# A decoder step of two layers with a KV cache: another root for the layer norms, a closing norm in one pass, and another order and form of the weight loads

## The chip, the cores and the metric

The kernel runs on one core of a Trainium2 chip. Times are device microseconds (us) of one launch, from the start of the program to its end. The core has five engines with queues of their own: PE (TensorE, matrix products), DVE (VectorE), ACT (ScalarE), POOL (GpSimd) and SP (SyncE, which here only issues DMAs). They meet through semaphores. All DMAs of the core share 16 DMA engines.

## What is computed

There are 8 sequences (batches) with one new token each, a model width of 512, 32 query heads of 128 on 8 key/value heads, and caches of 8192 positions in bfloat16. An attention block and a dense block are applied twice, with the same weights and the same caches:

```
def attention(x):                       # x: [8, 1, 512]
    q = x @ wq                          # wq: [512, 4096]
    scores = q . k_cache * 128 ** -0.5  # k_cache: [8, 8, 8192, 128]
    o = softmax(scores) . v_cache       # v_cache: [8, 8, 8192, 128]
    return o @ wo                       # wo: [4096, 512]

def dense(x):
    return silu(x @ w1) @ w2            # w1: [512, 1792], w2: [1792, 512]

layernorm(x) = (x - mean(x)) / sqrt(var(x) + 1e-5)

for layer in (0, 1):
    x = x + attention(layernorm(x))
    x = x + dense(layernorm(x))
```

The caches hold 268 MB. What the second layer reads again must be loaded again, unless it was kept on the chip.

## The kernel before

**Tasks and positions.** The work is cut into 128 tasks, one for each layer, batch and key/value head. A task has 8 positions of 1024 cache rows; position p belongs to task p // 8. K and V come in granules of 512 KB (two positions each). At each position PE transposes a part of K with an identity matrix (`emit_t`, L527; DVE or ACT copies the result back, L535 and L533), multiplies queries with K (`emit_s`, L566), and, 12 positions later, weights with V (`emit_pv`, L632). The softmax of a task lies between: a maximum on DVE (L577), an all-reduce over the partitions on POOL (L581), the exponential on ACT (L591), another all-reduce (L599), a transposition on PE (L607).

**The arena.** Cache granules live in an arena of 28 slots. The 20 granules of K of a batch that belong to heads 3 to 7 (the "kept" ones) have homes in slots 8 to 27: they stay, transposed, from layer 0 to layer 1 of a batch, whose tasks for these heads follow each other closely. So the order of tasks is 3 heads and 5 kept heads of batch 0, three heads of the next batches, the 5 kept heads of batch 0 in layer 1, and so on.

**The planner.** `plan_loads` puts all cache loads into a heap ordered by need, the position that first wants the data. It takes the loads out one by one and gives each a slot. The key for choosing prefers a slot that comes free at least 10 us (in the planner's own clock) ahead of the need, then the least waste, then the slot that comes free last. A load of several granules that finds no such slot is split. Each load gets `after`, the position at which its slots are free (-2: from the start). A slot with a home may be lent out only if the home's next load comes 10 us or more after the lent slot is free.

**The queue.** SP issues the loads strictly in the planner's order. After the commands of position p, `issue_until(p)` issues the loads at the head of the queue whose `after` is at most p; the first one that is not yet due holds up all behind it. At the start (L502 to L506) come the four granules of task 0, then `wq`, then what `after` = -2 allows at the head of the queue (two granules), then `wo`, `w1` and `w2` in one go. The input x is the first DMA of SP's queue (L464).

**Layer norm.** `normed` (L692) is used twice, at the opening (with wq) and at the closing (with w1). It sums x over the partitions (`total`, L674 on DVE and L676 on POOL), subtracts the mean (L680), starts the product with the weights on PE (L728), and meanwhile computes the sum of the squares of the centred x, again with an all-reduce. `inverse_root` (L652) then gets the inverse root on DVE: a guess by integer arithmetic (3 instructions) and three Newton steps (9 instructions). `scaled` (L710) multiplies the product by it.

**Chains.** For each batch, when its last head of layer 0 is done, `chain_of` (L817) takes that one batch from attention to the queries of layer 1: `wo`, residual, norm, `w1`, Silu by exponential and reciprocal, `w2`, residual, norm, `wq`. It is a list of steps, of which one or two are emitted at each position, beside the attention of other batches. The norms' stages (`ln_stages`, L684) lie beside pieces of the products: `ask` for the first heads is cut into as many pieces as the norm has stages. Before the first chain, from position 24, `column_sums` (L807) multiplies wq and w1 by ones.

**Closing.** `closing` (L765) handles the last dense block for all batches: residual (L759), rows by PE (L771), `normed` with w1, each product repeated four times over, six filler matmuls (`keep_busy(AFTER)`, L547), scaling (L710), Silu on ACT (L784), w2 on PE (L771), a copy (L788) and four DMAs (L966). A small Silu ahead of it (L778) makes ACT load the table for it.

Of the kernel before, what the change touches and what calls it, by code (L numbers as in the profile page):

```python
# [6 lines left out]
HQ = 32  # L7
DH = 128
SM_SCALE = DH ** -0.5
LN_EPS = 1e-5  # L10
RSQRT_SEED = float(0x5F3759DF)
NEWTON = 3

GRP = 8
GPT = 8
# [18 lines left out]
W1PARTS = 7  # L34
W2PARTS = 4
QSOON = 3
ASKS = (2, 5)
SUMS = 24
NTP = 3
NSCP = 2  # L40
NQB = 2
NST = 2
# [3 lines left out]
PVN = (12, 16)  # L46
CW = 32
AGAIN = 4
BEFORE, AFTER = 4, 6
ACT_EVAC = (0, 4, 6)  # L50

BF16 = mybir.dt.bfloat16
FP32 = mybir.dt.float32
INT32 = mybir.dt.int32
ACT = mybir.ActivationFunctionType
ALU = mybir.AluOpType
AX = mybir.AxisListType
# [140 lines left out]
def plan_loads(tasks, kept, nslot, ngran):  # L198
# [9 lines left out]
    heap = []  # L208
# [17 lines left out]
    for i, (layer, b, g) in enumerate(tasks):  # L226
# [11 lines left out]
        for ks in split(list(range(ngran)), wide):  # L238
            push("V", i, tuple(ks))

    def lead(need, after):
        return clock[max(0, need)] - clock[after] if after >= 0 else FAR

# [2 lines left out]
    loads = []  # L246
    while heap:
        d = heapq.heappop(heap)[-1]
        n = len(d.ks)
        if d.home is not None:  # L250
            for m in range(n):
                reserved[d.home + m].pop(0)
        else:
            best = None
            for slot in range(nslot - n + 1):
                held = free[slot:slot + n]
                if any(r and lead(r[0], f) < AHEAD for r, f in zip(reserved[slot:slot + n], d.free)):
# [35 lines left out]
def _build(ctx, nc, A_x, A_k_cache, A_v_cache, A_wq, A_wo, B_w1, B_w2, out):  # L293
# [67 lines left out]
    Xr = P  # L361
# [2 lines left out]
    Pf = P[:, :].bitcast(FP32)  # L364
    halves = (1 + FT + 1) // 2
    assert NST == 2 and 2 * KT <= FT <= HQ
    small = sb([128, 4 * B + 4 * REP * NST + USED + 2 * FT + 2 * HQ + NST + 1 + halves], FP32, "small")
    taken = [0]

    def cut(n):  # L370
        taken[0] += n
        return small[:, taken[0] - n:taken[0]]

    yr, tr, s1, s1a = [cut(B) for _ in range(4)]
# [85 lines left out]
    with nc.Block() as block:  # L460

        @block.sync
        def _(sync_eng):
            dma(sp, Xr[0:B, :], x_in, wsem["x"], writes=["P"])  # L464

            op(pool, lambda: pool.memset(ident[:, :], 1.0), writes=["ident"])
            op(
# [4 lines left out]
                ),  # L472
                reads=["ident"], writes=["ident"],
            )
            for n in range(NQB):
                op(pool, lambda n=n: pool.memset(QB[n], 0.0), writes=[f"QB{n}"])
            op(dve, lambda: dve.memset(one, 1.0), writes=["one"])
# [8 lines left out]
               reads=["hm"], writes=["far"])  # L486

            queue = list(loads)

            def issue_until(pos):  # L490
                while queue and queue[0].after <= pos:
                    issue(queue.pop(0))
# [4 lines left out]
            def load_rest():  # L497
                dma(sp, wo_sb[:, :, :], A_wo.rearrange("(h p) d -> p h d", p=128), wsem["wo"], writes=["wo"])
                dma(sp, w1_sb[:, :, :], B_w1.rearrange("(kt p) f -> p kt f", p=128), wsem["w1"], writes=["w1"])
                dma(sp, w2_sb[:, :, :], B_w2.rearrange("(ft p) d -> p ft d", p=128), wsem["w2"], writes=["w2"])  # L500
# [141 lines left out]
            def emit_norm(ti):  # L642
# [4 lines left out]
                else:  # L647
                    dst, rd = QA[:, b * HQ + g * REP:b * HQ + (g + 1) * REP], f"QA{b}"
                op(dve, lambda: dve.tensor_tensor(dst, OTp[ob][:, 0:REP * width_of(ti):width_of(ti)], rcp[st], ALU.mult),
                   reads=[f"OT{ob}", f"rcp{st}"], writes=[rd])  # L650

            def inverse_root(n):  # L652
                v, y, t = s1a[:, 0:n], yr[:, 0:n], tr[:, 0:n]
                vi, yi = v.bitcast(INT32), y.bitcast(INT32)

                def guess():
                    op(dve, lambda: dve.tensor_scalar(v, v, 1.0 / D, LN_EPS, op0=ALU.mult, op1=ALU.add),
                       reads=["s1a"], writes=["s1a"])
                    op(dve, lambda: dve.tensor_scalar(yi, vi, 1, None, op0=ALU.logical_shift_right),
                       reads=["s1a"], writes=["yr"])  # L660
                    op(dve, lambda: dve.tensor_scalar(yi, yi, -1.0, RSQRT_SEED, op0=ALU.mult, op1=ALU.add),
                       reads=["yr"], writes=["yr"])

                def newton():
                    op(dve, lambda: dve.tensor_tensor(t, y, y, ALU.mult), reads=["yr"], writes=["tr"])
                    op(dve, lambda: dve.scalar_tensor_tensor(t, t, -0.5, v, op0=ALU.mult, op1=ALU.mult),
                       reads=["tr", "s1a"], writes=["tr"])
                    op(dve, lambda: dve.scalar_tensor_tensor(y, t, 1.5, y, op0=ALU.add, op1=ALU.mult),
                       reads=["tr", "yr"], writes=["yr"])

                return [guess] + [newton] * NEWTON

            def total(xv, rx, n):
                op(dve, lambda: dve.tensor_reduce(s1[:, 0:n], xv.rearrange("p k b -> p b k"), AX.X, ALU.add),  # L674
# [17 lines left out]

                return [lambda: total(xv, rx, 1), second] + inverse_root(1)

            def normed(xv, rx, w_sb, rw, outs, again=1):

                total(xv, rx, B)
                center(xbB, ["PT", "xb"], xv, rx, B)
                for f in project(w_sb, rw, outs, KT, lambda k: xbB[:, k, :], "xb", B, again=again):
                    f()  # L700
                if again > 1:
                    keep_busy(AFTER)
# [12 lines left out]
            def project(w_sb, rw, outs, kparts, rhs_of, r_rhs, n, parts=1, again=1):  # L715

                steps = []
                w = CW if n == 1 else n * again

                def moved(k):  # L720
                    if n == 1:
                        return rhs_of(k).to_broadcast([128, w])
                    return rhs_of(k).unsqueeze(1).to_broadcast([128, again, n]) if again > 1 else rhs_of(k)

                for i, o in enumerate(outs):
                    for k in range(kparts):
                        steps.append(
                            lambda i=i, o=o, k=k: pe.matmul(  # L728
                                MISC[:, i * n:i * n + w] if again == 1 else
                                MISC[:, i * w:(i + 1) * w].rearrange("p (r b) -> p r b", b=n),  # L730
                                w_sb[:, k, o * 128:(o + 1) * 128], moved(k),
                                start=(k == 0), stop=(k == kparts - 1),
                            )
                        )
# [30 lines left out]
            def closing(x0, x1, r0, r1):  # L765
# [3 lines left out]
                def quads(lhs_of, rhs_of, parts, first, last):  # L769
# [14 lines left out]
                op(act, lambda: act.activation(hsB, hB, ACT.Silu), reads=["P"], writes=["hsB"])  # L784
# [32 lines left out]
            def chain_of(b):  # L817
# [179 lines left out]
```

## Time and profile before

| what | value |
|---|---|
| median of 3 runs | 1169.84 us (1167.94 to 1170.11) |
| the profiled execution: time, and its span | 1167.9 us, 1166.2 us |
| busy: PE, weight loads, DVE, ACT, POOL | 965.2, 753.7, 597.4, 382.7, 117.7 us |
| read from HBM | 465.05 MB, 399 GB/s over the span |
| granted PE clock, mean | 0.969 |
| cache loads: V of 512 KB, V of 1 MB, K of 512 KB, K of 1 MB, K of 2 MB | 284, 114, 192, 32, 24 |
| K and V copies out of transposition: DVE, ACT | 690 ns x 440, 1011 ns x 264 |

How to read it: busy time is a share of the span for each engine, and several engines work at once, so the shares don't add up to the time. The page has the span in 40 slices with the share of busy time as a digit from 0 to 9, and for the DMA engines the rate. The chain of work that ended last is followed back from the last instruction, at each step to what released it. In a timeline each line has a start, a duration, the engine, the line of the kernel, the operation, what it writes and reads, the number of instructions, and in brackets the idle time ahead of it with what ended it; "issue" there means that the profile shows nothing that the engine waited for. Times in a timeline count from the start of the span.

### The profile page before, as it was taken

Reading aid. Unit: us, or ns where it says so; the run is one execution under the profiler, and the core shown is the slowest. Engines: PE = TensorE matmul, PEld = TensorE weight load, DVE = VectorE, ACT = ScalarE, POOL = GpSimd, SP = SyncE. Lnnn points to the kernel's source line nnn. Section 1 sums busy time; section 2 is a strip of 40 time slices with the busy share of each in tenths; the row PEclk is TensorE's granted clock in tenths of the full one; section 3 lists DMA queues with packets and bytes.
Section 4 is the critical chain, followed back from the end, with each engine's and each line's share of the span. In section 5 each row is a group of like instructions: output and inputs, shape, how many; then the busy total and the mean of one; then the engine's idle time right before and its main releaser. Section 6 shows DMA issues by size and latency. Waiting matters only on the chain.

```text
span 1166.2 us, 44949 instructions
## 1 busy us (share of the span) xinstructions
PE 965.2 (83%) x19898; PEld 753.7 (65%) x19898; DVE 597.4 (51%) x1932; ACT 382.7 (33%) x660; POOL 117.7 (10%) x300
## 2 busy tenths in 40 slices
PE   4478888798879887888878988989889888888786
PEld 3367666576657675667656766767667665767564
DVE  2235654455535563556545654556445553556444
ACT  1133331343223431443223431343233422443232
POOL 0000111000110111001110111001100011001110
PEclk8799999999998999999999999899989999999999
DMA  9999999999999999999999999999999999999995
GB/s 346 393 417 378 385 407 412 420 413 402 410 422 405 404 398 417 421 407 399 407 423 411 389 406 422 420 404 396 414 422 412 396 409 420 420 382 406 412 411 214
DMA packets 100274, 467.98 MB, mean 401 GB/s; under 512 B 10472, under 2 KB 16368, under 8 KB 77808
## 3 DMA queue, kind: packets, MB, share of 16 engines
q1 hardware_dynamic: 100048, 465.10, 99.2%
q8 instruction: 157, 2.57, 0.9%
q14 instruction: 37, 0.30, 0.1%
q10 hardware_dynamic: 32, 0.00, 0.0%
HBM read 465.05 MB, written 0.01 MB: 399 GB/s over the span
## 4 chain that ended last, share of the span: by engine, by line
DMA 55%; PE 32%; DVE 5%; issue 4%; ACT 2%; SPq 1%; POOL 1%; POOLq 0%; ACTq 0%; DVEq 0%
DMA arena<-in_A_v_cache_dram 28%; DMA arena<-in_A_k_cache_dram 26%; PE TPp L527 12%; PE OTp L632 9%; PE SCp L566 6%; PE MISC L728 3%; ACT P L591 2%; PE TPp L607 2%; DVE small L577 2%; PE MISC L747 1%; DVE arena L535 1%; SPq L432 1%; POOL small L581 1%; DVE PT L611 0%; DVE small L579 0%
## 5 line engine op out<-in xcount | busy, mean ns | idle before, releaser
L527 PE MATMUL TPp<-ident,arena 128*128 128x128 bf16 x5632 | 444.9, 223 | 86.4 <-DMA arena<-in_A_k_cache_dram 80.7
L535 DVE COPY arena<-TPp 128x1024 bf16<-128x1024 bf16 x440 | 303.6, 690 | 311.9 <-PE TPp L527 309.7
L527 PEld LDWEIGHTS TPp<-ident,arena 128*128 128x128 bf16 x5632 | 330.8, 99 | 152.5 <-DMA arena<-in_A_k_cache_dram 99.1
L533 ACT COPY arena<-TPp 128x1024 bf16<-128x1024 bf16 x264 | 266.9, 1011 | 313.3 <-PE TPp L527 313.2
L632 PE MATMUL OTp<-PT,arena 128*128 128x64 bf16 (+1 forms) x8192 | 319.5, 191 | 56.9 <-DMA arena<-in_A_v_cache_dram 29.9
L632 PEld LDWEIGHTS OTp<-PT,arena 128*128 128x128 bf16 x8192 | 275.2, 98 | 96.6 <-issue 52.8
L566 PE MATMUL SCp<-arena,QB 128*32 128x512 bf16 x2048 | 208.6, 398 | 11.7 <-DVE arena L535 5.8
L591 ACT ACTIVATE P<-SCp,small 128x512 bf16<-128x512 f32 x128 | 87.9, 687 | 383.7 <-DVE small L587 218.5
L581 POOL PARTITION_ALL_REDUCE small<-small x128 | 47.5, 371 | 718.9 <-DVE small L579 691.6
L577 DVE TENSOR_REDUCE small<-SCp 128x1 f32<-128x512 f32 x128 | 87.5, 684 | 40.6 <-PE SCp L566 39.7
L566 PEld LDWEIGHTS SCp<-arena,QB 128*32 128x32 bf16 x2048 | 54.3, 93 | 59.6 <-DVE arena L535 9.6
L599 POOL PARTITION_ALL_REDUCE small<-small x128 | 55.8, 436 | 235.3 <-DVE small L597 235.3
L611 DVE COPY PT<-TPp 128x256 bf16<-128x256 bf16 x128 | 37.3, 292 | 81.4 <-PE TPp L607 81.4
L607 PE MATMUL TPp<-ident,P 128*128 128x128 bf16 x512 | 51.3, 223 | 24.4 <-ACT P L591 24.3
L607 PEld LDWEIGHTS TPp<-ident,P 128*128 128x128 bf16 x512 | 29.2, 98 | 57.3 <-ACT P L591 44.9
L597 DVE TENSOR_SCALAR small<-small 128x4 f32<-128x4 f32 x128 | 29.1, 228 | 31.4 <-ACT P L591 30.3
L728 PE MATMUL MISC<-XT,wq 128*128 128x32 bf16 x1024 | 39.9, 177 | 1.4 <-issue 1.3
L728 PEld LDWEIGHTS MISC<-XT,wq 128*128 128x128 bf16 x1024 | 32.2, 96 | 9.0 <-issue 9.0
L747 PE MATMUL MISC<-at,wo 128*128 128x32 bf16 x1024 | 35.8, 176 | 0.9 <-issue 0.9
L747 PEld LDWEIGHTS MISC<-at,wo 128*128 128x128 bf16 x1024 | 31.5, 96 | 4.8 <-issue 4.8
L579 DVE SCALAR_TENSOR_TENSOR small<-small 128x4 f32<-128x4 f32 x128 | 28.5, 223 | 4.5
L585 DVE SCALAR_TENSOR_TENSOR small<-small 128x4 f32<-128x4 f32 x128 | 19.9, 156 | 20.4 <-POOL small L581 20.4
(69 smaller groups left out, 321.1 us busy)
## 6 DMA issues: line engine op xcount, KB each, us to landing
arena<-in_A_v_cache_dram SPq DMA_DIRECT2D x284, 512.0 KB, 8.2
arena<-in_A_v_cache_dram SPq DMA_DIRECT2D x114, 1024.0 KB, 11.5
arena<-in_A_k_cache_dram SPq DMA_DIRECT2D x192, 512.0 KB, 8.2
arena<-in_A_k_cache_dram SPq DMA_DIRECT2D x24, 2048.0 KB, 14.0
arena<-in_A_k_cache_dram SPq DMA_DIRECT2D x32, 1024.0 KB, 12.8
wq<-in_A_wq_dram SPq DMA_DIRECT2D x1, 4096.0 KB, 16.9
wo<-in_A_wo_dram SPq DMA_DIRECT2D x1, 4096.0 KB, 30.4
w<-in_B_w_dram SPq DMA_DIRECT2D x2, 1792.0 KB, 25.2
```

The lines of the kernel that those rows point to most:

```text
L527: lambda c=c: pe.transpose(tpv[:, c, :], chunk(slot, h * GRP + c), ident[:, :])
L533: op(act, lambda: act.copy(dst, TPp[tb][:, :]), reads=[f"TP{tb}"], writes=[r_half(slot, h)])
L535: op(dve, lambda: dve.tensor_copy(dst, TPp[tb][:, :]), reads=[f"TP{tb}"], writes=[r_half(slot, h)])
L566: lambda c=c: pe.matmul(SCp[bank][c * QUAD:(c + 1) * QUAD, :], QB[qn][:, NGRAN - 1 - k:NGRAN - 1 - k + QUAD], ARENA[:, slot * SLOT + c * K ...
L577: op(dve, lambda: dve.tensor_reduce(rowmax, SCp[bank][:, :], AX.X, ALU.max), reads=[f"SC{bank}"], writes=["rowmax"])
L581: op(pool, lambda: pool.partition_all_reduce(tops, top, 128, bass.bass_isa.ReduceOp.max), reads=["top"], writes=["tops"])
L591: op(act, lambda: act.activation(P[:, :], SCp[bank][:, :], ACT.Exp, bias=shift, scale=SM_SCALE, accum_out=rs[st]), reads=[f"SC{bank}", "sh ...
L599: op(pool, lambda: pool.partition_all_reduce(ssa[st], ssm[st], 128, bass.bass_isa.ReduceOp.add), reads=[f"ssm{st}"], writes=[f"ssa{st}"])
L607: lambda c=c: pe.transpose(tpv[:, c, :], P[:, c * 128:(c + 1) * 128], ident[:, :])
L632: lambda c=c, cc=cc: pe.matmul(otp, chunk(slot, h * GRP + c), pv[:, cc % CPB, cc // CPB % NQ, k, :].unsqueeze(2).to_broadcast([128, REP, w ...
L728: lambda i=i, o=o, k=k: pe.matmul(MISC[:, i * n:i * n + w] if again == 1 else MISC[:, i * w:(i + 1) * w].rearrange("p (r b) -> p r b", b=n ...
L747: lambda o=o, h=h: pe.matmul(MISC[:, o * w:(o + 1) * w], wo_sb[:, h, o * 128:(o + 1) * 128], rhs_of(h).to_broadcast([128, w]) if n == 1 el ...
```

## The change

- Every inverse root becomes exp(-0.5 ln(v)) on ACT, behind one DVE instruction that forms the variance. ACT loads, at the start, a table that holds both Ln and Exp. The chains' norms have four stages for six; the pieces of `ask` stay six.
- The closing's norm is done in one pass: ACT squares x, DVE sums x and the squares, and one all-reduce on POOL takes both sums. POOL then forms the offset and the centred x itself, two operations of kinds that it does not have elsewhere. Three DVE instructions form the variance. Two filler matmuls come ahead of w1's product, five behind it. The last Silu becomes Exp on ACT and three operations on DVE.
- w2 is loaded with two of its rows side by side in a partition (packets of 2 KB for 1 KB). To match, w1's columns are read with a step of two.
- wo, w1 and w2 go into the planner's heap at positions 16, 30 and 48 instead of into the queue at the start. The loads of the first three tasks take the slot that is free earliest; as `after` is the first part of this key, their loads of V are always split into single granules.
- x is loaded by ACT's queue.

```diff
+WEIGHTS = (("wo", 16), ("w1", 30), ("w2", 48))
-BEFORE, AFTER = 4, 6
+BEFORE, BETWEEN, AFTER = 4, 2, 5
...
+    for kind, need in WEIGHTS:
+        heapq.heappush(heap, (need, kind, 0, (), Load(kind, 0, 0, 0, (), need, [], None)))
...
+        if n == 0:
+            d.after = -2
+            loads.append(d)
+            continue
...
+                elif d.task < OPENING:
+                    key = (after, waste, 0, slot)
...
-            dma(sp, Xr[0:B, :], x_in, wsem["x"], writes=["P"])
+            dma(act, Xr[0:B, :], x_in, wsem["x"], writes=["P"])
...
+            act.add_instruction(mybir.InstLoadActFuncSet(
+                name=nc.get_next_instruction_name(), act_func_set_id=LN_EXP, ins=[], outs=[]))
...
+                        if d.kind == "w2":
+                            dst = dst[:, :, :].rearrange("p (a c) d -> p a (c d)", c=FC)
+                            src = src.rearrange("(a p c) d -> p a (c d)", p=128, c=FC)
...
-            load_rest()
...
+            def root(n):
+                op(act, lambda: act.activation(tr[:, 0:n], s1a[:, 0:n], ACT.Ln), reads=["s1a"], writes=["tr"])
+                op(act, lambda: act.activation(yr[:, 0:n], tr[:, 0:n], ACT.Exp, scale=-0.5), reads=["tr"], writes=["yr"])
...
-                return [guess] + [newton] * NEWTON
+                return [shifted, lambda: root(n)]
...
+                def columns(k, o):
+                    if rw == "w1":
+                        lo = o // FC * FC * 128 + o % FC
+                        return w_sb[:, k, lo:lo + FC * 127 + 1:FC]
+                    return w_sb[:, k, o * 128:(o + 1) * 128]
...
-                op(act, lambda: act.activation(raw[:, 0:1], raw[:, 0:1], ACT.Silu), reads=["raw"], writes=["raw"])
...
-                normed(x1, r1, w1_sb, "w1", range(FT), AGAIN)
+                op(act, lambda: act.activation(sqB, x1, ACT.Square), reads=[r1], writes=["PT", "sqB"])
+                op(dve, lambda: dve.tensor_reduce(s1, x1.rearrange("p k b -> p b k"), AX.X, ALU.add),
+                   reads=[r1], writes=["two"])
+                op(dve, lambda: dve.tensor_reduce(two[:, B:2 * B], sqB.rearrange("p k b -> p b k"), AX.X, ALU.add),
+                   reads=["sqB"], writes=["two"])
+                op(pool, lambda: pool.partition_all_reduce(twoa, two, 128, bass.bass_isa.ReduceOp.add),
+                   reads=["two"], writes=["twoa"])
+                op(pool, lambda: pool.tensor_scalar(offB, s1a, -1.0 / D, None, op0=ALU.mult), reads=["twoa"], writes=["offB"])
+                op(pool, lambda: pool.tensor_tensor(
+                    xbB, offB.unsqueeze(1).to_broadcast([128, KT, B]), x1, ALU.add),
+                   reads=["offB", r1], writes=["PT", "xb"])
+                keep_busy(BETWEEN)
+                project(w1_sb, "w1", range(FT), KT, lambda k: xbB[:, k, :], "xb", B, again=AGAIN)[0]()
+                keep_busy(AFTER)
...
+                root(B)
                 scaled(hB.rearrange("p (f b) -> p f b", b=B), ["P"], FT, AGAIN)
-                op(act, lambda: act.activation(hsB, hB, ACT.Silu), reads=["P"], writes=["hsB"])
+                op(act, lambda: act.activation(ehB, hB, ACT.Exp, scale=-1.0), reads=["P"], writes=["ehB"])
+                op(dve, lambda: dve.tensor_scalar(ehB, ehB, 1.0, None, op0=ALU.add), reads=["ehB"], writes=["ehB"])
+                op(dve, lambda: dve.reciprocal(ehB, ehB), reads=["ehB"], writes=["ehB"])
+                op(dve, lambda: dve.tensor_tensor(hsB, hB, ehB, ALU.mult), reads=["P", "ehB"], writes=["hsB"])
...
-                pieces, asked = ask(first, soon, len(norm))
+                pieces, asked = ask(first, soon, Q3PARTS)
```

More of the change, by code (lines that the diff above doesn't have):

```diff
@@ L10 @@
 LN_EPS = 1e-5
-RSQRT_SEED = float(0x5F3759DF)
-NEWTON = 3
 GRP = 8
@@ L36 @@
 QSOON = 3
+Q3PARTS = 6
 ASKS = (2, 5)
 SUMS = 24
+FC = 2
+LN_EXP = 6
+OPENING = 3
+WEIGHTS = (("wo", 16), ("w1", 30), ("w2", 48))
 NTP = 3
@@ L53 @@
 FP32 = mybir.dt.float32
-INT32 = mybir.dt.int32
 ACT = mybir.ActivationFunctionType
@@ L366, in _build @@
     assert NST == 2 and 2 * KT <= FT <= HQ
-    small = sb([128, 4 * B + 4 * REP * NST + USED + 2 * FT + 2 * HQ + NST + 1 + halves], FP32, "small")
+    small = sb([128, 7 * B + 4 * REP * NST + USED + 2 * FT + 2 * HQ + NST + 1 + halves], FP32, "small")
     taken = [0]
@@ L372, in cut @@
         return small[:, taken[0] - n:taken[0]]
-    yr, tr, s1, s1a = [cut(B) for _ in range(4)]
+    yr, tr = [cut(B) for _ in range(2)]
+    two, twoa = [cut(2 * B) for _ in range(2)]
+    s1, s1a = two[:, 0:B], twoa[:, 0:B]
+    offB = cut(B)
     ssm, rcp, ssa, other = zip(*[[cut(REP) for _ in range(4)] for _ in range(NST)])
@@ L488, in _ @@
             queue = list(loads)
+            weights = {"wo": (A_wo, wo_sb), "w1": (B_w1, w1_sb), "w2": (B_w2, w2_sb)}
             def issue_until(pos):
                 while queue and queue[0].after <= pos:
-                    issue(queue.pop(0))
+                    d = queue.pop(0)
+                    if d.kind in weights:
+                        src, dst = weights[d.kind]
+                        if d.kind == "w2":
+                            dst = dst[:, :, :].rearrange("p (a c) d -> p a (c d)", c=FC)
+                            src = src.rearrange("(a p c) d -> p a (c d)", p=128, c=FC)
+                        else:
+                            dst, src = dst[:, :, :], src.rearrange("(k p) n -> p k n", p=128)
+                        dma(sp, dst, src, wsem[d.kind], writes=[d.kind])
+                    else:
+                        issue(d)
             def load_wq():
                 dma(sp, wq_sb[:, :, :], A_wq.rearrange("(kt p) n -> p kt n", p=128), wsem["wq"], writes=["wq"])
[L497 to L500, printed above, removed]
             while len(k_slot) < NGRAN:
@@ L650, in emit_norm, with shifted @@
                    reads=[f"OT{ob}", f"rcp{st}"], writes=[rd])
+            def root(n):
+                op(act, lambda: act.activation(tr[:, 0:n], s1a[:, 0:n], ACT.Ln), reads=["s1a"], writes=["tr"])
+                op(act, lambda: act.activation(yr[:, 0:n], tr[:, 0:n], ACT.Exp, scale=-0.5), reads=["tr"], writes=["yr"])
             def inverse_root(n):
[L653 to L657, printed above, removed]
+                def shifted():
+                    op(dve, lambda: dve.tensor_scalar(s1a[:, 0:n], s1a[:, 0:n], 1.0 / D, LN_EPS, op0=ALU.mult, op1=ALU.add),
                        reads=["s1a"], writes=["s1a"])
[L659 to L669, printed above, removed]
-                return [guess] + [newton] * NEWTON
+                return [shifted, lambda: root(n)]
             def total(xv, rx, n):
@@ L693, in ln_stages, with normed @@
                 return [lambda: total(xv, rx, 1), second] + inverse_root(1)
-            def normed(xv, rx, w_sb, rw, outs, again=1):
+            def normed(xv, rx, w_sb, rw, outs):
                 total(xv, rx, B)
                 center(xbB, ["PT", "xb"], xv, rx, B)
-                for f in project(w_sb, rw, outs, KT, lambda k: xbB[:, k, :], "xb", B, again=again):
+                for f in project(w_sb, rw, outs, KT, lambda k: xbB[:, k, :], "xb", B):
                     f()
-                if again > 1:
-                    keep_busy(AFTER)
                 center(xcB, ["xcB"], xv, rx, B)
@@ L730, in project @@
                                 MISC[:, i * w:(i + 1) * w].rearrange("p (r b) -> p r b", b=n),
-                                w_sb[:, k, o * 128:(o + 1) * 128], moved(k),
+                                columns(k, o), moved(k),
                                 start=(k == 0), stop=(k == kparts - 1),
@@ new lines, in closing @@
+                project(w1_sb, "w1", range(FT), KT, lambda k: xbB[:, k, :], "xb", B, again=AGAIN)[0]()
+                keep_busy(AFTER)
+                sqa, m2 = twoa[:, B:2 * B], tr[:, 0:B]
+                op(dve, lambda: dve.scalar_tensor_tensor(m2, s1a, 1.0 / D / D, s1a, op0=ALU.mult, op1=ALU.mult),
+                   reads=["twoa"], writes=["tr"])
+                op(dve, lambda: dve.scalar_tensor_tensor(sqa, sqa, 1.0 / D, m2, op0=ALU.mult, op1=ALU.subtract),
+                   reads=["twoa", "tr"], writes=["sqa"])
@@ L783, in closing @@
+                op(dve, lambda: dve.tensor_scalar(s1a, sqa, 0.0, LN_EPS, op0=ALU.max, op1=ALU.add),
+                   reads=["sqa"], writes=["twoa", "s1a"])
+                root(B)
                 scaled(hB.rearrange("p (f b) -> p f b", b=B), ["P"], FT, AGAIN)
-                op(act, lambda: act.activation(hsB, hB, ACT.Silu), reads=["P"], writes=["hsB"])
+                op(act, lambda: act.activation(ehB, hB, ACT.Exp, scale=-1.0), reads=["P"], writes=["ehB"])
+                op(dve, lambda: dve.tensor_scalar(ehB, ehB, 1.0, None, op0=ALU.add), reads=["ehB"], writes=["ehB"])
```

## The prediction

> **What bounds the kernel now.** I read the slices of the page, the chain of work that ended last, busy time in stretches of 10 us with the DMA queue's waits beside it, and last GpSimd's timeline and that of the end.
>
> ```profile
> DMA  9999999999999999999999999999999999999995
> GB/s 346 393 417 378 385 407 412 420 413 402 410 422 405 404 398 417 421 407 399 407 423 411 389 406 422 420 404 396 414 422 412 396 409 420 420 382 406 412 411 214
> DMA 55%; PE 32%; DVE 5%; issue 4%; ACT 2%; SPq 1%; POOL 1%; POOLq 0%; ACTq 0%; DVEq 0%
> ```
>
> The DMA engines are busy in every slice but the last, and the chain runs mostly through cache loads. An edit between the first byte and the last counts by what it does to this stream alone. What lies behind the last V load (landed at 1155.56 in the chain) counts in full: 10.6 us. One stretch of the stream is poor:
>
> ```profile
> 90.00:100.00 10.00, 8.28 (x190) 6.95 (x190) 4.94 (x14) 3.45 (x6) 0.80 (x2) 1.00 1.02 424
> 100.00:110.00 10.00, 9.37 (x206) 7.94 (x202) 5.65 (x14) 4.38 (x7) 0.80 (x2) 1.00 0.94 367
> 110.00:120.00 10.00, 8.03 (x167) 6.54 (x165) 4.96 (x14) 3.80 (x6) 0.80 (x2) 1.00 0.94 345
> 120.00:130.00 10.00, 8.87 (x161) 6.63 (x159) 6.31 (x17) 3.81 (x6) 1.17 (x3) 1.00 0.93 345
> 130.00:140.00 10.00, 9.12 (x212) 7.53 (x211) 5.98 (x22) 3.91 (x6) 1.21 (x3) 1.00 1.02 406
> ```
>
> ```profile
> SPq L106 <- PE OTp L632: 50.3, 17, 12.7
> ```
>
> The last three columns of the stretches are granted clock, DMA share and GB/s. The line below them is SP's wait, from 70 to 135 us, for PV matmuls to give up V slots (50.3 us in 17 waits): PE is late there. SP's timeline says why: after six K granules and wq come wo, w1 and w2, the next K is issued at 30.91 and lands at 46.6. The softmax maxima (L577) of tasks 0 to 8 stand at 30.0, 55.3, 68.0, 79.1, 90.4, 101.4, 110.1, 120.1 and 128.5: PE loses some 16 us behind the weights, the arena fills, and the queue runs dry later.
>
> ```profile
> 0.78 0.20 POOL L466 MEMSET ident<- 128x128 bf16 x1 [0.29 <-POOLq L982]
> 9.87 0.28 POOL L469 TENSOR_SCALAR_AFFINE_SELECT ident<-ident 128x128 bf16<-128x128 bf16 x1 [8.88 <-issue]
> 10.12 0.18 POOL L476 MEMSET QB<- 128x35 bf16 x2
> 19.88 0.43 POOL L676 PARTITION_ALL_REDUCE small<-small  x1 [9.58 <-issue]
> 21.20 0.40 POOL L676 PARTITION_ALL_REDUCE small<-small  x1 [0.90 <-DVE small L674]
> ```
>
> GpSimd stood 8.88 us before its affine select and 9.58 us before its first all-reduce, both "issue": it waited for nothing that the profile shows. The all-reduce's input was there at 17.50, so at least 2.38 us of the second are no wait for data. Each gap is ahead of the first operation of another kind; memsets have none, and no all-reduce behind another has one.
>
> ```profile
> 1157.59 0.41 POOL L676 PARTITION_ALL_REDUCE small<-small  x1 [4.48 <-DVE small L674]
> ...
> 1158.28 1.66 PE L728 MATMUL MISC<-PT,w 128*128 128x32 bf16 x56 [0.74 <-DVE PT L680]
> ...
> 1159.78 2.49 PE L547 MATMUL TPp<-wq,ident 128*128 128x512 bf16 x6
> ...
> 1161.82 0.28 DVE L710 TENSOR_TENSOR P<-MISC,small 128x112 f32<-128x112 f32 x1
> 1162.13 0.30 ACT L784 ACTIVATE PT<-P 128x112 bf16<-128x112 f32 x1 [8.29 <-DVE P L710]
> 1162.48 0.95 PE L771 MATMUL SCp<-w,PT 128*8 128x128 bf16 x56 [0.21 <-ACT PT L784]
> ```
>
> This is the end: sum, w1, six filler matmuls beside the root, scaling, Silu, w2. GpSimd has one kind of work in it.
>
> **Part 1: weights by need, -4.15 us.** Now the third load past wq reuses slot 0 and waits for position 1 (lines 488 to 506), so the weights fill the time. With the new key the first three tasks take free slots. Worked by hand through the planner: 18 granules, wq and wo are issued before the first load that waits (the kept K of task 3, for position 14). That is 17.8 MB. The stretches of before had moved 16.0 MB by 45 us, so the DMAs have work until about 49. Position 8 stays at 30; at the 8.4 to 11.2 us a task seen above position 14 comes at 36 to 38, at half clock (granted in 35 to 50 us) near 44, in time. Further on, positions 24, 32, 40 and 64 come when the K granule that each needs has landed: 19.9, 26.0, 30.2 and 43.0 MB at 420 GB/s (380 in w1 and w2) and 1.5 us for landing give about 56, 71, 82 and 112 (before 68, 79, 90, 120), 7 us or more ahead of the time when the DMAs run out. So the hole closes: (41+63+63) GB/s x 10 us = 1.67 MB, at 408 GB/s **-4.1 us**. By the DMA share (0.94 for 1.03) it is 2.7, by 424 GB/s 5.1: these are the ends. What is late next is the stream itself.
>
> x moves from SP's queue to ACT's: K starts at 0.79 for 1.23, **-0.44**; x is wanted at 10.3. w2 in rows of 2 KB: 1.84 MB at the 376 GB/s of 40 to 45 us would take 4.9 us, at the 407 of 4 KB rows 4.5; I take **-0.2** of 0 to -0.4. Against it, the new key cuts the V loads of three tasks into single granules: 6.3 MB at 407 GB/s (130 to 160 us) for 423 (210 to 230 us, pairs), **+0.6**.
>
> **Part 2: roots of the chains, 0.** Sixteen times 11 DVE instructions of 0.15 us go (26 us), and 32 ACT ones of 0.2 us come. The chains lie where the DMA share is 1.03 at 408 GB/s (130 to 170 us), and their steps are spread by position; the stream hides both. The new wait is Ln's, on DVE; behind it in ACT's queue stand evacuations (L533) and the softmax exponential, for which PE waits. At the opening, DVE's twelve end at 24.02, but wq's 128 matmuls end at 24.24 on PE, and scaling needs both: 0. I keep -1 to +1. Table loads cost 1.28 us each in the trace; the one ahead of Silu (1152.35) lay beside PV work: 0. Ln and Exp exchanging tables would cost two loads a root, off the path as long as w1 is later than the root (below).
>
> **Part 3: the closing, +9.4 us.** From x1 at 1157.26. Square on ACT: 0.03 + 0.22 (0.20 for one column, 0.30 for 112); DVE's sum of it 0.03 + 0.21, ending 1157.75; the all-reduce of 16 columns 0.09 + 0.43 (0.41 for 8), ending 1158.27. Now GpSimd goes from all-reduce to tensor_scalar and tensor_tensor, kinds that it has not run. Lower end of their gap: 0; upper end: 9.58 for each kind. I take one gap of 8.9, the row with less DMA traffic beside it: to 1167.17. offB and xbB at 0.2 and 0.25 (memset 0.10, affine select 0.28) with 0.13 between: w1 starts at 1167.75, for 1158.28 before. The root on DVE and ACT, some 1.2 us behind the all-reduce, is hidden by this wait. w1 1.66, to 1169.41; scaling, Exp and three DVE operations (0.28 + 0.30 + 3 x 0.27 and gaps) give hsB at 1170.95. But five fillers of 0.42 stand ahead of w2 on PE, to 1171.5: w2 starts +9.05. After 9 us without work PE may run it at half clock (0.95 more); I add 0.35. The two filler matmuls in between end long before. w1's weights are now read with a step of two: 56 loads took 1.56 us; from 0 to twice that, I take 0, as the row's matmuls are as long.
>
> The Trainium skill, GPSIMD Engine Reference, section 2.1 Instruction dispatch, says that the first call into freshly loaded code costs about 6 us and shows no instruction of its own. The two gaps of 8.88 and 9.58 look like that and are longer; by the page's figure the closing would cost 6.5 and the forecast would be some 3 us lower. The same skill, TensorE: Matmul & The Clock Gate, section Weight-path perf modes, says that fast weight loads take strided columns; no run here shows it.
>
> **Sum.** -4.1 - 0.44 - 0.2 + 0.6 + 9.4 = **+5.25 us**. On the profiled execution's 1167.9 that is 1173.2. That one lies at the low end of the runs, 1.9 below their median 1169.84; I put the forecast between the two, at **1174.0**.
>
> **Rivals.**
> *No gap on GpSimd* (change of kind costs nothing outside the start). For it: both gaps lie in the first 20 us, where much else starts. Against: the second begins at 10.3, with GpSimd already running. Then w1 starts 0.55 late, fillers end at 1162.6 for 1162.48: closing +0.15 (-0.4 at full clock), total -4.0: **1165**, faster. Chance 0.12.
> *The hole does not close*: the queue stands at a load that waits for a position while the arena is not yet used up, and PE catches up no sooner. It decides if position 14 comes after 49 us. For it: PE is at half clock from 35 to 50 us now. Against: 5 to 12 us of margin. Closing +9.4 and nothing gained: **1178**, slower. Chance 0.08.
> *A gap for each of the two kinds*: 8.9 more, **1183**, slower. Chance 0.06. For it: affine select and all-reduce each paid. Against: nothing shows whether the two new kinds share one.
> *The forecast*, one gap and the hole closed: 0.74, with its own range 1169 to 1177.5 from the ends above (opening -2.7 to -5.6, closing +6 to +10.5).
>
> Range 1167 to 1179: the forecast's case, the dearer opening, and a part of the cheap closing. A measurement of this kernel can tell about 0.2% (2.3 us) from no change. Faster: 0.12 less a little that ends near 1168, with a tail of the forecast, 0.12. Same: a tenth of the forecast's case and that little, 0.10. Slower: 0.78.
>
> **What would show it.** Right: before offB a POOL idle of 6 to 10 us on "issue"; w1's matmuls in the closing some 9.5 us behind the sum; 405 GB/s or more from 90 to 130 us; L577 of tasks 1 to 7 about 8 to 16 us earlier; last V load landing about 4 us earlier. Wrong: offB within 0.1 us of the all-reduce's end (then the kernel is faster); a stretch under 380 GB/s in 20 to 130 us besides the weights; table loads between Ln and Exp; 128x128 weight loads of w1 above 0.06 us apart.

## The result, and the profile after

The changed kernel takes 1172.6 us (median of 6 runs, 1171.81 to 1174.11), the kernel before 1168.68 (6 runs, 1167.94 to 1170.11): a ratio of 1.0031, 95% interval 1.0016 to 1.0046, so slower by 3.6 us or so (between 1.9 and 5.4). The profiled execution took 1172.31 us with a span of 1170.6, which is 4.4 more than the span of before. DVE is busy for 571.4 us (26.0 less), ACT for 388.6 (5.9 more). The saving on DVE does not show in the time.

The slices of the changed kernel's page, and its chain of work that ended last:

```profile
DMA  9999999999999999999999999999999999999993
GB/s 367 389 419 395 406 407 406 422 410 392 413 424 411 402 399 423 419 395 407 409 423 405 400 409 422 415 391 407 407 422 408 407 398 423 413 406 385 413 410 118
...
DMA 59%; PE 28%; SPq 5%; DVE 3%; issue 3%; ACT 2%; POOL 1%; ACTq 0%; POOLq 0%; DVEq 0%
```

The slices hold both halves of the answer. Of the 40, the first ones are faster (367 GB/s for 346 in the first; 395 and 406 in the fourth and fifth for 378 and 385), and the last is half empty: 118 for 214. What the stream gains at the start is lost behind its end.

The stretches in which the hole was, changed kernel (the last three columns are granted clock, DMA share, GB/s), and SP's wait there for PV matmuls, from 70 to 135 us:

```profile
100.00:110.00 10.00, 9.64 (x168) 8.09 (x164) 4.76 (x12) 3.43 (x7) 0.37 (x1) 0.77 1.00 404
110.00:120.00 10.00, 9.47 (x193) 7.69 (x190) 5.87 (x16) 4.84 (x8) 1.23 (x3) 1.00 0.99 367
120.00:130.00 10.00, 7.70 (x144) 5.73 (x139) 4.50 (x13) 3.60 (x6) 0.80 (x2) 1.00 1.02 406
```

```profile
SPq L108 <- PE OTp L653: 28.5, 15, 5.4
```

404, 367 and 406 GB/s stand for 367, 345 and 345, and SP waits 28.5 us for 50.3. By 150 us the DMAs have moved 59.25 MB for 57.71, which is 1.54 MB or 3.8 us of the stream. The last V load lands at 1151.61 for 1155.56: 3.95 us earlier.

The end of the changed kernel (timeline, all engines):

```profile
1153.12 0.19 DVE L776 TENSOR_TENSOR XT<-MISC,XT 128x32 bf16<-128x32 f32 x1 [0.68 <-PE MISC L764]
...
1153.95 0.48 POOL L803 PARTITION_ALL_REDUCE small<-small  x1 [4.79 <-DVE small L801]
...
1161.25 0.27 POOL L805 TENSOR_SCALAR small<-small 128x8 f32<-128x8 f32 x1 [6.82 <-issue]
1161.60 0.25 POOL L806 TENSOR_TENSOR PT<-small,XT 128x32 bf16<-128x32 f32 x1
1161.62 0.25 DVE L817 TENSOR_SCALAR small<-small 128x8 f32<-128x8 f32 x1 [6.79 <-POOL small L805]
...
1161.90 1.67 PE L745 MATMUL MISC<-PT,w 128*128 128x32 bf16 x56 [7.77 <-POOL PT L806]
...
1163.41 2.29 PE L568 MATMUL TPp<-wq,ident 128*128 128x512 bf16 x5
...
1164.50 0.85 DVE L823 RECIPROCAL P<-P 128x112 f32<-128x112 f32 x1
...
1165.39 0.28 DVE L824 TENSOR_TENSOR PT<-P 128x112 bf16<-128x112 f32 x1
...
1165.72 1.11 PE L788 MATMUL SCp<-w,PT 128*8 128x128 bf16 x56
...
1167.21 1.73 SPq L1006 DMA_DIRECT2D out_dram<-P  x2
```

Here is the loss in one number: 6.82 us between the all-reduce and the offset, on "issue", with PE, DVE and ACT standing behind it. From the residual (1153.12) to w2's start it is 12.60 us, for 5.41 before; from the residual to the end of the span 17.48 for 9.13, **+8.35**. With the 3.95 gained this is the +4.4 of the span.

One thing was not expected at all. GpSimd at the start of the changed kernel:

```profile
0.79 0.20 POOL L480 MEMSET ident<- 128x128 bf16 x1 [0.29 <-POOLq L1022]
1.28 0.29 POOL L483 TENSOR_SCALAR_AFFINE_SELECT ident<-ident 128x128 bf16<-128x128 bf16 x1 [0.29 <-POOL ident L480]
...
12.36 0.43 POOL L688 PARTITION_ALL_REDUCE small<-small  x1 [10.64 <-DVE small L686]
```

The 8.88 us ahead of the affine select are gone; the same instruction now runs at 1.28. Nothing in the change touches it. The all-reduce comes at 12.36 for 19.88.

### The profile page after: what moved, and what is told of

It is laid out like the page before. It is cut to its first block, busy times and chain, and to the rows that moved or that the text cites. A ratio compares the mean times of both kernels' runs of the same rounds, so it can differ in the third digit from the quotient of the medians.

```text
span 1170.6 us, 44813 instructions
## 1 busy us (share of the span) xinstructions
PE 967.5 (83%) x19899; PEld 755.6 (65%) x19899; DVE 571.4 (49%) x1736; ACT 388.6 (33%) x695; POOL 118.3 (10%) x301
## 3 DMA queue, kind: packets, MB, share of 16 engines
q8 instruction: 157, 2.57, 0.9%
## 4 chain that ended last, share of the span: by engine, by line
DMA 59%; PE 28%; SPq 5%; DVE 3%; issue 3%; ACT 2%; POOL 1%; ACTq 0%; POOLq 0%; DVEq 0%
DMA arena<-in_A_k_cache_dram 33%; DMA arena<-in_A_v_cache_dram 26%; PE TPp L548 9%; PE OTp L653 8%; PE SCp L587 5%; SPq L446 5%; PE MISC L745 2%; ACT P L612 2%; PE TPp L628 2%; PE MISC L764 1%; DVE small L598 1%; POOL small L602 1%; DVE PT L632 0%; DVE small L600 0%; DVE small L606 0%
## 5 line engine op out<-in xcount | busy, mean ns | idle before, releaser
L600 DVE SCALAR_TENSOR_TENSOR small<-small 128x4 f32<-128x4 f32 x128 | 28.5, 223 | 4.5
```

## The experiments

**1. Centring back on DVE.** Is the whole loss GpSimd's gap, and does the one-pass closing gain anything without it? The changed kernel with one instruction in place of GpSimd's two:

```diff
-                op(pool, lambda: pool.tensor_scalar(offB, s1a, -1.0 / D, None, op0=ALU.mult), reads=["twoa"], writes=["offB"])
-                op(pool, lambda: pool.tensor_tensor(
-                    xbB, offB.unsqueeze(1).to_broadcast([128, KT, B]), x1, ALU.add),
-                   reads=["offB", r1], writes=["PT", "xb"])
+                op(dve, lambda: dve.scalar_tensor_tensor(
+                    xbB, s1a.unsqueeze(1).to_broadcast([128, KT, B]), -1.0 / D, x1, op0=ALU.mult, op1=ALU.add),
+                   reads=["twoa", r1], writes=["PT", "xb"])
```

> The changed kernel with the closing's centring back on DVE (one operation for the two on GpSimd); all else as changed. Switch theory (GpSimd holds the code of one group of operations, all-reduce in one, tensor_scalar and tensor_tensor in another, and a change of group costs 7 to 10 us): the 6.8 us ahead of the offset vanish and some 0.6 us of GpSimd work and handover with them; in all 7 to 8 us less than the changed kernel, 1164.5 to 1165.5, which is 3 to 4 us faster than before. As the program then ends in all-reduces, the gap of about 9 us ahead of the affine select at the start comes back, where it costs under 0.5 us. Rival (the one-pass closing is long by itself, its longer chain through ACT, DVE and the fillers): at most 2 us less than the changed kernel, 1170.5 or more.

Measured: 1165.14 us (11 runs), ratio to before 0.9977 (0.9966 to 0.9988), so 7.5 us below the changed kernel by the medians and 6.3 by the two ratios. The end, and GpSimd's start, in this kernel:

```profile
1157.06 0.19 DVE L776 TENSOR_TENSOR XT<-MISC,XT 128x32 bf16<-128x32 f32 x1 [0.69 <-PE MISC L764]
...
1158.41 0.19 DVE L805 SCALAR_TENSOR_TENSOR PT<-small,XT 128x32 bf16<-128x32 f32 x1 [0.60 <-POOL small L803]
...
1161.26 0.85 DVE L822 RECIPROCAL P<-P 128x112 f32<-128x112 f32 x1
...
1162.48 0.96 PE L788 MATMUL SCp<-w,PT 128*8 128x128 bf16 x56
```

```profile
10.33 0.28 POOL L483 TENSOR_SCALAR_AFFINE_SELECT ident<-ident 128x128 bf16<-128x128 bf16 x1 [9.34 <-issue]
...
20.14 0.42 POOL L688 PARTITION_ALL_REDUCE small<-small  x1 [9.37 <-issue]
```

From the residual to w2 it is now 5.42 us, for 5.41 before the change: the one-pass closing gains nothing, and all of its loss goes with GpSimd's two instructions. Of the 7.19 us ahead of w2 the gap itself is 6.82; the longer w2 (0.96 now, 1.11 in the changed kernel) and the slower end of the output are gone too. At the start both gaps are back, at 9.34 and 9.37, though only GpSimd's two instructions at the very end differ. (The profiled execution is this kernel's slowest, 1167.8 us: the stream loses about 4 us between tasks 52 and 64, far from the edit, which is why its end stands late.)

**2. The loads alone.** The kernel before with wo, w1 and w2 in the planner's heap, the new slot key and x on ACT's queue; w2 in rows of one, old roots, old closing.

```diff
+OPENING = 3
+WEIGHTS = (("wo", 16), ("w1", 30), ("w2", 48))
...
+                elif d.task < OPENING:
+                    key = (after, waste, 0, slot)
...
-            dma(sp, Xr[0:B, :], x_in, wsem["x"], writes=["P"])
+            dma(act, Xr[0:B, :], x_in, wsem["x"], writes=["P"])
...
-            load_rest()
```

> The kernel before with the loads of the changed one alone: weights by need, the first three tasks in the slots that are free earliest, x on ACT's queue (w2 still in rows of one). Theory (part 1 of the prediction): 4 us less than before (3 to 5), about 1164.7, with the hole from 100 to 130 us closed but for one stretch, last V load landing near 1151.6. Rival (the earlier last load in the changed kernel comes from the DVE time that the Newton steps gave up): within 1 us of before.

Measured: 1165.69 us (12 runs), ratio 0.9974 (0.9963 to 0.9985): 3.0 us, between 1.8 and 4.3, the low end of the 3 to 5 that I expected. In its stretches the hole is closed:

```profile
100.00:110.00 10.00, 9.35 (x160) 7.33 (x157) 4.91 (x13) 3.62 (x7) 0.80 (x2) 0.85 1.01 412
110.00:120.00 10.00, 9.24 (x190) 7.49 (x186) 5.81 (x15) 4.37 (x7) 0.80 (x3) 1.00 1.02 405
120.00:130.00 10.00, 8.07 (x156) 6.31 (x154) 4.57 (x13) 3.92 (x6) 0.80 (x2) 1.00 1.03 408
```

Its softmax maxima come earlier from task 8 on, by 3.9 us in the median (2.1 to 5.4), and they stay earlier to the end: the last V load lands at 1151.22, 4.34 earlier than before. This is the gain, alone.

**3. Need without key, and key without need.** Which half of the loads does it? One kernel has the weights by need and x on ACT's queue, with the old slot key; the other has the new key and nothing else:

```diff
+                elif d.task < OPENING:
+                    key = (after, waste, 0, slot)
```

> The kernel before with the weights by need and x on ACT's queue, but the old key for slots. Theory (the key makes the gain, since it frees the queue's head at the start): after six K granules and wq, 7.3 MB that are in by about 21 us, the next load waits for position 1 near 26 us, with no weights to fill the time; the DMAs stand idle some 5 us between 20 and 27, and what the closed hole gives (4 us) is lost again: 1168 to 1171, within 0.3% of before. Rival (the gain is in the weights' later place alone): 3 to 4 us less than before, about 1165.

> The kernel before with the new key for slots alone (weights in one go at the start, x on SP's queue). Theory: the start then issues 18 granules ahead of the weights, so most of what part 1 does happens without the heap's part: 2 to 4 us less than before, 1164.5 to 1166.5, with task 2's maximum (L577) near 62 us, between the 68 of before and the 57 of the changed kernel. Rival (the weights' place alone): within 1 us of before.

Weights by need alone: 1174.92 us, ratio 1.0050 (1.0038 to 1.0063), slower by 5.9, and so worse than the 1168 to 1171 that I expected. Its stretches, and the issue of one load by SP:

```profile
20.00:30.00 10.00, 7.51 (x163) 5.72 (x164) 4.00 (x18) 1.31 (x3) 0.82 (x2) 0.59 0.32 95
30.00:40.00 10.00, 7.19 (x110) 5.13 (x108) 4.91 (x12) 3.19 (x6) 0.83 (x2) 0.90 0.88 308
```

```profile
3.69 23.35 SPq L440 DMA_DIRECT2D arena<-in_A_k_cache_dram  x3
```

The third K behind wq wants slot 0 and waits for position 1; by the trace SP waits 21.9 us there for PE's score matmuls. Before, the weights stood ahead of that wait and kept the DMAs busy; now nothing does, and the queue runs dry (95 GB/s between 20 and 30 us). From task 8 on the tasks are late by some 7 us in the median. The key alone gave 1168.06, ratio 0.9990 (0.9982 to 0.9999): 1 us, less than the 2 to 4 that I expected, and under what I count as a difference. Its trace says why:

```profile
24.93 21.24 SPq L435 DMA_DIRECT2D w<-in_B_w_dram  x2
46.28 7.30 SPq L435 DMA_DIRECT2D arena<-in_A_k_cache_dram  x1
```

The 18 granules run ahead, then w1 and w2 follow wo in one go, and the kept K of task 3 has its turn only at 46.28; in the changed kernel that is at 39.27, ahead of w1 and w2. So PE starves again, and the hole stays (360, 345 and 384 GB/s from 100 to 130 us). Alone the halves give +5.9 and -1.0 us, together -3.0: neither does it without the other. By the traces, the key makes the room that the spread weights need, and the spread keeps K flowing.

**4. The roots alone.** Ln and Exp at the opening and in the chains, in the kernel before; the closing keeps Newton.

```diff
+                def root():
+                    op(act, lambda: act.activation(tr[:, 0:n], s1a[:, 0:n], ACT.Ln), reads=["s1a"], writes=["tr"])
+                    op(act, lambda: act.activation(yr[:, 0:n], tr[:, 0:n], ACT.Exp, scale=-0.5), reads=["tr"], writes=["yr"])
...
-                return [lambda: total(xv, rx, 1), second] + inverse_root(1)
+                return [lambda: total(xv, rx, 1), second] + by_log(1)
```

> The kernel before with the roots of the opening and of the sixteen norms in the chains by Ln and Exp on ACT (the closing as before). Theory (part 2: the DMA stream hides them): within 1 us of before, with DVE's busy time some 25 us less, ACT's some 6.5 us more, and one table load at the start and one ahead of Silu. Rival (the Newton steps hold up evacuations and through them the release of slots): 2 us or more less than before. Other rival (Ln and Exp swap tables, or Ln holds up ACT's queue): 2 us or more above before.

Measured: 1167.89 us (11 runs), ratio 0.9985 (0.9976 to 0.9995), 1.7 us less, and so a little past the 1 us on either side that I had allowed, but below the 0.2% that I count. Its trace shows no place for a gain: from task 8 on the maxima stand 0.35 us later than before in the median (single tasks up to 2 earlier and 3 later), and the last V load lands at 1155.95 for 1155.56. Whether the roots gain a microsecond stays open; that they cost nothing is shown.

**5. What the gap follows.** The prediction said that GpSimd pays ahead of the first operation of another kind. With the start gap gone from the changed kernel, that can't be all of it. A new theory: all-reduce is in one group of operations, and tensor_scalar, tensor_tensor and the affine select are in another; every change of group costs a gap, and a launch begins in the group in which the one before it ended. Two kernels test it, both the kernel before with an unused tensor_scalar on GpSimd, behind the last all-reduce of the program or at two positions in the middle:

```diff
+                op(pool, lambda: pool.tensor_scalar(idle, hm, 1.0, None, op0=ALU.mult), reads=["hm"], writes=["idle"])
```

```diff
+                if p in (416, 664):
+                    op(pool, lambda: pool.tensor_scalar(idle, hm, 1.0, None, op0=ALU.mult), reads=["hm"], writes=["idle"])
```

> The kernel before with one added tensor_scalar on GpSimd behind the last all-reduce, 128x4, whose result nobody uses. Switch theory, with the start in whatever group the program ended in: the gap ahead of the affine select at the start (8.88 us) is gone, the affine select starts near 1.3, and a gap of about 7 us stands ahead of the added operation at the end, beside the root and w2; the operation ends near 1166.5, so the time is that of before within 1 us. Rival (every first operation of a kind costs once): the gap at the start stays at 8.9, and the added one has a gap of its own.

> The kernel before with two added tensor_scalars on GpSimd, 128x4, unused, at positions 416 and 664, each between two all-reduces of the softmax. Switch theory: four gaps of 7 to 10 us, ahead of each of the two and ahead of each all-reduce that follows; the softmax is late by up to 18 us each time, the DMAs' lead covers some 10 of it, so 5 to 20 us slower. Rival (first use): one gap, ahead of the first of the two, none ahead of the all-reduces and none ahead of the second; under 3 us slower.

At the end: 1168.84 us, ratio 1.0009 (0.9999 to 1.0018), no difference in time that can be told. GpSimd of that kernel:

```profile
1.28 0.29 POOL L470 TENSOR_SCALAR_AFFINE_SELECT ident<-ident 128x128 bf16<-128x128 bf16 x1 [0.29 <-POOL ident L467]
...
12.96 0.43 POOL L677 PARTITION_ALL_REDUCE small<-small  x1 [11.25 <-DVE small L675]
...
1167.37 0.26 POOL L784 TENSOR_SCALAR small<-small 128x4 f32<-128x4 f32 x1 [7.10 <-issue]
```

One idle instruction at the end takes the gap away from the start and has 7.10 us ahead of itself. The gap on the way back to the all-reduce does not show at the start: GpSimd had 11.25 us there, up to the sum that it waited for, in which it could lie. In the middle, 1188.37 us, ratio 1.0169 (1.0147 to 1.0191):

```profile
509.36 0.26 POOL L931 TENSOR_SCALAR small<-small 128x4 f32<-128x4 f32 x1 [10.84 <-issue]
516.57 0.44 POOL L600 PARTITION_ALL_REDUCE small<-small  x1 [6.95 <-issue]
...
788.98 0.26 POOL L931 TENSOR_SCALAR small<-small 128x4 f32<-128x4 f32 x1 [10.53 <-issue]
795.26 0.44 POOL L600 PARTITION_ALL_REDUCE small<-small  x1 [6.02 <-issue]
```

Each idle instruction costs two gaps, one to get there and one back, although both groups had already run in this launch. "First use" is refuted; "change of group" stands. Two instructions that nobody reads cost 20 us, the upper end of the 5 to 20 expected: each holds GpSimd for 17 us or so, and the softmax of every task needs it twice. From 495 to 525 us this kernel moves 290 GB/s for 407, from 775 to 805 it moves 264 for 401; that is 7.6 MB, or 19 us.

**6. The output's last microsecond.** In the changed kernel 3.4 us pass from the issue of the output's DMAs to the end of the span, 2.4 before and 2.3 in experiment 1. Is it that the queues had been quiet for long? Experiment 1 with 22 filler matmuls ahead of w2 for 5:

```diff
-BEFORE, BETWEEN, AFTER = 4, 2, 5
+BEFORE, BETWEEN, AFTER = 4, 2, 22
```

> The kernel with centring on DVE (e1_dve), with 22 filler matmuls ahead of w2 in place of 5. It takes the gap on GpSimd away and puts a wait of about the same length in its place: 17 more fillers of 0.42 us, 7.1 us, so that the output's DMAs are again issued some 15 us behind the last cache load, as in the changed kernel (15.6 us there; 7 to 10 us in all the others). Theory (the output's DMAs are slow because the queues have moved nothing for long): their issue takes about 1.6 us for 0.7, and 3.4 us pass from issue to the end of the span, for 2.3. Rival (they are slow because of what GpSimd does): 0.7 us and 2.3 us, as in e1_dve. The closing is some 6 to 7 us longer than in e1_dve either way, as far as the fillers outlast the root, the scaling and Silu.

```profile
1157.10 5.26 PE L568 MATMUL TPp<-wq,ident 128*128 128x512 bf16 x22
...
1162.29 0.95 PE L788 MATMUL SCp<-w,PT 128*8 128x128 bf16 x56
...
1163.62 0.73 SPq L1005 DMA_DIRECT2D out_dram<-P  x2
```

The output was issued in 0.73 us, and 2.3 us passed from its issue to the end of the span, at 1165.9. But the pause came out short: the fillers took 0.24 us each, not 0.42, at a granted clock of 1.00 from 1158 to 1162 us. The output was issued 11.1 us behind the matmuls on the last V load for 15.6 in the changed kernel (8.2 before). So a pause of 11 us did not do it here. Nor is a long pause, or a gap on GpSimd beside it, needed. The kernel of experiment 5 with the idle instructions in the middle has the closing of before, no gap at its end, and its output issued 8.6 us behind the matmuls on the last V load:

```profile
1186.04 1.26 SPq L969 DMA_DIRECT2D out_dram<-P  x2
```

Its span ends at 1189.1, 3.1 us after that issue. So most of the microsecond is there without either cause, and what it follows stays open. The times of the kernel with 22 fillers are 1168.08 us, ratio 1.0002 (0.9988 to 1.0016), with no more in them than the longer end.

**7. A version that beats both.** Experiment 1, with the last Silu as Silu again (its table loaded behind the root), two fillers ahead of w2 for five, and V in pairs also in the first three tasks:

```diff
-            if n > 1 and (best is None or -best[0] < EARLIEST[n]):
+            if n > 1 and (best is None or n > 2 or d.task >= OPENING and -best[0] < EARLIEST[n]):
...
+                op(act, lambda: act.activation(raw[:, 0:1], raw[:, 0:1], ACT.Silu), reads=["raw", "yr"], writes=["raw"])
...
+                op(act, lambda: act.activation(hsB, hB, ACT.Silu), reads=["P"], writes=["hsB"])
```

> The changed kernel with the closing's centring on DVE, the last Silu again by its own table (loaded behind the root, beside w1's product), two fillers for five behind w1, and pairs of V granules kept in the first three tasks. Theory: 7.5 us less than the changed kernel for GpSimd as in the run with DVE's centring, 1.0 to 1.3 less for the closing (Silu's one instruction of 0.30 for Exp and three on DVE of 1.35, of which a reciprocal of 0.85), 0 to 0.6 less for the pairs: 1163 to 1164.2, 4 to 5 us faster than before. Rival (the fillers are needed): w2's product at half clock, 0.95 us become 1.6, and little is left of the gain in the closing.

```profile
1153.64 0.19 DVE L776 TENSOR_TENSOR XT<-MISC,XT 128x32 bf16<-128x32 f32 x1 [0.68 <-PE MISC L764]
...
1156.17 1.28 ACT L819 ACT_TABLE_LOAD   x1
...
1157.90 0.95 PE L788 MATMUL SCp<-w,PT 128*8 128x128 bf16 x56 [0.28 <-ACT PT L821]
```

Measured: 1164.44 us (5 runs), ratio 0.9960 (0.9946 to 0.9973), 4.6 us less than before. From the residual to w2 it is 4.26 us for 5.42: the table load lies beside w1's matmuls, and the reciprocal is gone. By the intervals it is not told apart from experiment 1.

## Why the prediction was right

It was right in the terms that decide, a gap on GpSimd on the path and a closed hole in the stream, and wrong in what it took the gap to follow. The sum was close: 1173.2 for the profiled execution, which took 1172.31, and 1174.0 for the runs, which gave 1172.6. In part that is luck, as two misses in the closing have opposite signs. Point by point:

- **The opening, -4.15.** Right: -3.95 by the last V load in the changed kernel, -3.0 (1.8 to 4.3) by the runs of experiment 2. The path by hand held in its times: the kept K of task 3 went out at 39.27 (position 14 was forecast for 36 to 44). By the trace it hardly waited for position 14: the issue of one K granule ahead of it lasted from 17.07 to 36.70, and SP came to the kept K only at 39.2. The softmax maxima of tasks 2, 3, 4 and 7 stand at 57.5, 73.1, 83.0 and 115.7, for 56, 71, 82 and 112. Against those of before, the maxima of tasks 1 to 7 came 2.7 to 17.7 us earlier, not 8 to 16. The term for V was too large: by the pages only three pairs (3.1 MB, not 6.3) more are cut, which at the prediction's own rates is 0.3 us for 0.6. The terms for x and for w2's rows were not measured by themselves. Not foreseen: the second stretch reached only 367 GB/s, which I had named as a sign against me; its DMA share is 0.99, so the queues were hardly dry, and experiment 2 has 405 there with the same loads but for w2's rows. That the key and the spread need each other was half seen, in the cover that the weights gave to slot 0; that the key gives little without the spread I did not see.
- **The roots of the chains, 0.** Right within what can be told, with the open microsecond of experiment 4. No table load stands between Ln and Exp: they take 0.21 us each, and the one load for both lies at 1.4 us.
- **The closing, +9.4.** Measured +8.35, as the balance of several misses: -2.1 for the gap, -0.2 for half clock, +0.2 for fillers and handover, +1.0 for the output. *The gap*: 6.82 us for 8.9 taken; it is the mis-sized term. The rows at hand (8.88 and 9.58) were of gaps beside DMA traffic (267 GB/s in the first 10 us, 409 in the next). Beside traffic the two gaps ahead of a tensor_scalar in experiment 5 took 10.84 and 10.53; without it they took 6.82 (changed kernel) and 7.10 (experiment 5, at the end). That traffic makes this difference was not tested, and the two gaps on the way back, 6.95 and 6.02, were short beside traffic. The Trainium skill, GPSIMD Engine Reference, section 2.1 Instruction dispatch, gives some 6 us for the first call into freshly loaded code, with no instruction shown. The measurement at the end is nearer to that figure than to the rows that I used, though the page speaks of a first call and experiment 5 shows the price at each change. *The reciprocal*: 0.85 us for 0.27. It could have been read before: rows of 4 and 14 columns at 170 and 242 ns give 7 ns a column, hence some 0.95 us for 112. The Trainium skill, VectorE: DVE Perf Modes, section First, the fixed hardware budget, says that the reciprocal is an iterative divide with a repeat count of 8; no run here shows that. In the changed kernel it costs nothing, as the five fillers end at 1165.70 and it lets w2 start at 1165.72; in experiment 1 it sets w2's start. *The output's DMAs*: +1.0 that I had not counted (experiment 6).
- **Half clock.** I had put 0.35 for it; w2 took 1.11 us for 0.95, and the granted clock was 0.50 from 1156 to 1166 us, all through the gap and the fillers that were to prevent it. The gap need not be the reason that I gave: experiment 1, without it, was granted 0.50 from 1156 to 1162, and with the closing of before w2 took 0.95 or 0.96 us in five kernels, but 1.60 and 1.30 in the two of experiment 5.
- **The root under cover.** Right in effect, wrong in time. I had it done about 1.2 us behind the all-reduce. DVE's last instruction of the variance (L817) writes the sums that GpSimd still had to read, so it waited until 1161.62, and the root came at 1162.36. It is still ahead of w1's end at 1163.57, so it costs nothing.
- **w1 in steps of two.** Right: 1.67 us for 1.66. The Trainium skill, TensorE: Matmul & The Clock Gate, section Weight-path perf modes, says that fast weight loads take strided columns. The trace agrees in the time: the median load of w1 in the closing took 104 ns, in steps as without.
- **The reading of the two gaps** at the start, "the first operation of another kind", was the step that failed. The prediction came out right because the closing has one such gap under both readings. Under the one that the experiments bear out, the change also takes a gap from the start and puts one at the end. The first was all but hidden behind the loading of wq: wq landed at 20.2 us and its matmuls began at 20.68. The idle instruction at the end (experiment 5) removes this gap, and from task 8 on the maxima come no earlier in the median. Its runs alone would not tell, as its closing was also 0.7 us longer. The second gap lies on the path.

The rivals: a closing without a gap fell with the 6.82 us; a gap for each kind fell too, as the tensor_tensor follows the tensor_scalar without one; the hole that does not close fell with experiment 2.

## What to carry to other kernels

Two small operations moved to an engine that seems idle can cost more than hundreds of instructions saved elsewhere: here they cost about 7 us, where 26 us of DVE work saved gave less than 0.2%. Before work is moved to GpSimd, look at which operations it runs now, and keep those that share a group together; an idle time on "issue" ahead of a trivial instruction is the sign. When a part of a change reorders loads, ask which wait the loads that move had been covering; and size an instruction by two rows of its own kind, not by another kind of the same shape.

## What the runs showed of the hardware

- GpSimd pays for each change between all-reduce and tensor_scalar, tensor_tensor or affine select: 6.0 to 10.8 us (10.84, 6.95, 10.53 and 6.02 in mid-stream, 6.82 and 7.10 with the DMA queues at rest). Memsets have no such gap. No DMA packet shows in the changed kernel's gap, from 1154 to 1161 us, and the queues of kind "instruction" move 2.57 and 0.30 MB in the kernel before, in the changed one and in the one with four more changes of group; what the gap consists of isn't visible.
- In the kernels whose last GpSimd operation is tensor_scalar or tensor_tensor, the affine select at the start of the launch came at 1.28 us (two kernels); where it is an all-reduce, at 9.67 to 11.26 (nine kernels). That the launch before it sets this is inferred, as each trace holds a single launch.
- A filler matmul of 512 columns took 0.46 us at a granted clock of 0.50 (changed kernel), and 0.24 in the mean of a row of 22, most of them at 1.00 (experiment 6).
